# Three widths instead of four for TensorE's branches in the experts' products

## The chip, the cores and the metric

The kernel runs on one core of a Trainium2 chip. The metric is the device time of one execution in microseconds (us). Three runs of the kernel before took 733.88, 737.55 and 741.72 us; the median is 737.55 us. The execution that the profiler recorded took 735.24 us, of which 733.3 us lie between its first and its last instruction (the span).

## The reference, cut to what matters

Three parts follow each other. All data are 32-bit floats.

1. An attention over 4 batches, 8 heads, 576 positions and 64 values a head: a local one (each position sees the keys less than 4 away) plus one on fourfold averaged positions. Its result is x, 2304 tokens by 512.
2. A dense block without a gate: `h = ((x @ w1) * (x @ w2)) @ w3`, then `x = h @ w_out`.
3. A routed block with 8 experts, one expert a token:

```
logits = x @ w_gate                      # 2304 x 8
e_idx  = argmax(logits, axis=1)          # each token's one expert
gate_w = softmax(logits)[e_idx];  eom = sigmoid(x @ w_output_gate)
for e in range(8):
    mask = e_idx == e
    h  = relu(x[mask] @ w1[e])           # 512 -> 1024
    ye = h @ w2[e]                       # 1024 -> 512
    out[mask] = gate_w[mask] * eom[mask, e] * ye
```

How many tokens an expert gets is known only while the kernel runs.

## The kernel before, in words

**Stages.** The first 460 us or so make the attention, the dense block and the routing tables; the attention's small steps are spread between the matrix products. Then come the experts, from about 477 us to the end.

**Precision.** A product of two 32-bit matrices is made as three TensorE products of split operands: high by high, high by low, low by high (`mm3`, L419 to L421; `mm3n`, L425 to L427). Each of the three is one weight load (PEld) and one matmul (PE). The splitting is a cast on ScalarE (L775) and a subtraction on VectorE or GpSimd (L777).

**Experts by rank.** `route_rank` sorts the experts by their count. The program has eight ranks, and a rank r has a fixed capacity `CAPS[r]` in token columns: 352, 336, 320, 304, 288, 288, 272, and 384 for the last one, rank 7, which is the fullest expert. Tokens over a capacity are handled after the loop by `overflow`. The weights of a rank's expert are read by an address held in a register (`ew_load`, SP's queue), 4 MB a rank in eight transfers.

**First and second product.** `ga_pair(r, f0)` makes two of the eight 128-row parts of `relu(x @ w1)` for rank r: 2 parts x 4 slices of the inner dimension x 3 = 24 matmuls on one column range. `gb_step(r, dc)` makes one of the four 128-row parts of the second product: 8 slices x 3 = 24 matmuls. Ranks 1 to 7 call `ga_pair` four times each, ranks 0 to 6 call `gb_step` four times each (rank 7 ends with another form, `gb_rows`): 56 calls. I call the code of one such call a block. Rank 0's first product has no branches and lies before the loop.

**The branches.** Each block is made by `by_width`. It reads the rank's true count into a register of TensorE once a rank (`value_load`, L647), and writes the same 24 matmuls several times into the program, once for each entry of `CUTS`: for the full capacity C and for C less 16, 32 or 48 columns. Only the copy (arm) that the count calls for is executed. The first matmul of an accumulation always covers C columns, to clear the rest of the accumulator; the others have the arm's width.

```
CUTS = tuple(range(0, 64, 16))                       # L39
...
def arm(a, b):                                       # in by_width, from L649
    if b - a == 1:
        products(C - CUTS[a])
        return
    m = (a + b) // 2
    with tc.If(rt["n"][r] > C - CUTS[m]) as cond:    # L654
        arm(a, m)
    with cond.Else():
        arm(m, b)

arm(0, len(CUTS))
```

The branches are instructions of TensorE's queue alone; no other engine sees them. The order in the program is: compare with C-32; compare with C-16, arm C, jump to the end, arm C-16, jump to the end; compare with C-48, arm C-32, jump to the end, arm C-48. A count within 16 of C, or within 32 of it, costs two compares and one jump to the end; a smaller one costs two compares, both of which jump.

**Order.** From rank 0's second product on, the order of all five queues is written out by hand (`manual_schedule`): the second product of rank r, its blocks mixed with the transposes (L750) that prepare rank r+1's tokens, then the first product of rank r+1, its blocks mixed with the transposes of rank r's result (L861) and its scatter to the output (L851). ScalarE and VectorE take each block's result out of PSUM (L803 after the first product, L845 after the second). The weights of the coming ranks are loaded and split meanwhile.

Of the kernel before, what the change touches and what calls it, by code (L numbers as in the profile page):

```python
# [35 lines left out]
NBLK = [-(-c // P) for c in CAPS]  # L36
NBM = max(NBLK)
CMAX = max(CAPS)
CUTS = tuple(range(0, 64, 16))  # L39
NEG = -1e30  # L40
OOB = 1.0e6
RING = 2 * G
# [7 lines left out]
def attention_moe_kernel(ctx: ExitStack, tc: tile.TileContext, q, k, vw_in, v4_in, w1, w2, w3, w_out,  # L50
# [594 lines left out]
    def by_width(r, C, products):  # L645
# [3 lines left out]
        def arm(a, b):  # L649
# [11 lines that stand above are left out]
# [534 lines left out]
```

## Time and profile before

| What | Value |
|---|---|
| Median of three runs | 737.55 us (733.88 to 741.72) |
| Profiled execution | 735.24 us, span 733.3 us |
[...]
| TensorE matmuls busy | 687.4 us, 94% of the span |
| TensorE weight loads busy | 655.7 us, 89% (they overlap the matmuls) |
| VectorE, ScalarE, GpSimd busy | 382.6, 287.3 and 330.8 us |

The busy time of an engine is the union of its instructions; what is left of a stretch is idle time. In the view by stretches the columns are the stretch from:to, its length, the busy time of PE, PEld, DVE, ACT and POOL with the number of instructions, the granted clock, the busy share of the DMA engines and GB/s. A rank's stretch there runs from the start of its first product (rank 0: second) to the start of the next rank's, in us from the start of the span. "Idle before <- releaser" names what the profile takes for the end of the wait. Where an instruction waits for several semaphores, it names the one that moved last, which need not be the one that was waited for. Branches, register loads and waits are instructions of the sequencer that feeds an engine. They are not counted as busy, but their durations are recorded (PEldq is the sequencer of TensorE), and the sequencer runs ahead of its engine.

### The profile page before, as it was taken

The page shows a single profiled execution, that of the slowest core. Times are in us where ns is not written, and L with a number is a line of the kernel's source. Part 1 is how long each engine was busy: PE and PEld are TensorE (multiplying, and loading weights), DVE is VectorE, ACT ScalarE, POOL GpSimd, SP SyncE. Part 2 cuts the span into 40 slices and gives each one's busy share as a digit, 9 for nine tenths or more (in the row PEclk, how much of TensorE's full clock was granted, in tenths as well). Part 3 has the DMA queues.
Part 4 walks back from the last instruction along what each step waited for, and adds up shares of the span by engine and source line. Part 5 has one row for each costly group of instructions (what it writes and reads, how often), then busy time and mean ns, then how long its engine had stood idle before and what let it go on. Part 6 is the DMA issues. An engine that isn't in the chain of part 4 may idle for free.

```text
span 733.3 us, 14894 instructions
## 1 busy us (share of the span) xinstructions
PE 687.4 (94%) x5710; PEld 655.7 (89%) x5711; DVE 382.6 (52%) x887; ACT 287.3 (39%) x664; POOL 330.8 (45%) x339
## 2 busy tenths in 40 slices
PE   5689999999999999999999999989999998988995
PEld 3589989899999999999999999979989998987994
DVE  8889889854544545443243434462733445535340
ACT  3446435562543245145122120444444534544520
POOL 6868468763662255141011120243545546557331
PEclk9999999999999999999999999989999999999998
DMA  8879645463342043111100101573645647557301
GB/s 328 239 247 299 217 122 189 129 177 116 98 136 82 22 117 95 44 40 44 44 22 1 44 1 59 200 250 89 203 135 188 212 149 238 175 179 237 122 29 42
DMA packets 38297, 98.26 MB, mean 134 GB/s; under 512 B 6018, under 2 KB 12930, under 8 KB 38192
## 3 DMA queue, kind: packets, MB, share of 16 engines
q1 hardware_dynamic: 34768, 86.82, 37.4%
q0 software_dynamic: 3424, 9.93, 3.6%
q8 instruction: 79, 1.29, 0.7%
q14 instruction: 26, 0.21, 0.1%
HBM read 84.93 MB, written 12.29 MB: 133 GB/s over the span
## 4 chain that ended last, share of the span: by engine, by line
PE 67%; issue 9%; DVE 9%; POOL 7%; DMA 5%; ACT 1%; SPq 0%; POOLq 0%; DVEq 0%; ACTq 0%
PE g L419 14%; PE g L421 14%; PE g L420 14%; PE g L425 6%; PE g L426 5%; PE g L427 5%; POOL W L777 2%; PE at L282 2%; POOL out_dram L851 2%; DVE cv L139 2%; DMA v<-in_v_dram 1%; DVE cv L140 1%; PE at L210 1%; DMA kz<-in_k_dram 1%; DVE wf L141 1%
## 5 line engine op out<-in xcount | busy, mean ns | idle before, releaser
L419 PE MATMUL g<-xh,W 128*128 128x384 f32 x384 | 131.9, 343 | 0.6 <-ACT a L453 0.6
L421 PE MATMUL g<-xh,W 128*128 128x384 f32 x384 | 129.2, 337 | 0.8 <-POOL W L398 0.8
L420 PE MATMUL g<-xl,W 128*128 128x384 f32 x384 | 129.2, 336 | 0.0
L777 POOL TENSOR_TENSOR W<-raw,W 128x1024 fp32r<-128x1024 f32 x29 | 70.8, 2441 | 89.6 <-ACT W L775 89.6
L458 POOL TENSOR_TENSOR h<-a,h 128x384 fp32r<-128x384 f32 x30 | 30.5, 1018 | 100.3 <-ACT h L456 100.3
L419 PEld LDWEIGHTS g<-xh,W 128*128 128x128 f32 x384 | 72.1, 188 | 2.3 <-ACT a L453 1.2
L421 PEld LDWEIGHTS g<-xh,W 128*128 128x128 f32 x384 | 72.1, 188 | 1.7 <-POOL W L398 1.6
L425 PE MATMUL g<-xT,W 128*128 128x288 f32 (+5 forms) x224 | 68.8, 307 | 4.9 <-ACT W L775 3.2
L425 PE MATMUL g<-h,W 128*128 128x320 f32 (+7 forms) x224 | 68.4, 305 | 5.4 <-ACT xT L754 2.1
L420 PEld LDWEIGHTS g<-xl,W 128*128 128x128 f32 x384 | 72.2, 188 | 0.1
L419 PE MATMUL g<-wc,h 128*128 128x272 f32 (+1 forms) x240 | 68.7, 287 | 0.0
L420 PE MATMUL g<-wc,h 128*128 128x272 f32 (+1 forms) x240 | 68.3, 286 | 0.0
L421 PE MATMUL g<-wc,h 128*128 128x272 f32 (+1 forms) x240 | 67.8, 285 | 0.0
L427 PE MATMUL g<-xT,W 128*128 128x320 f32 (+4 forms) x224 | 66.4, 296 | 0.9 <-issue 0.9
L426 PE MATMUL g<-h,W 128*128 128x320 f32 (+4 forms) x224 | 66.1, 295 | 0.8 <-DVE h L803 0.8
L426 PE MATMUL g<-xT,W 128*128 128x320 f32 (+4 forms) x224 | 66.3, 296 | 0.0
L427 PE MATMUL g<-h,W 128*128 128x320 f32 (+4 forms) x224 | 66.0, 295 | 0.3 <-issue 0.3
L775 ACT CAST W<-raw 128x1024 fp32r<-128x1024 f32 x61 | 63.2, 1047 | 4.0 <-DMA raw<-in_moe_w_dram 4.0
L777 DVE TENSOR_TENSOR W<-raw,W 128x1024 fp32r<-128x1024 f32 x32 | 43.3, 1352 | 37.3 <-ACT W L775 37.3
L454 DVE TENSOR_TENSOR a<-g,a 128x384 f32<-128x384 f32 x48 | 26.7, 555 | 55.3 <-PE g L421 47.3
L803 DVE SCALAR_TENSOR_TENSOR h<-g,h 128x288 fp32r<-128x288 f32 (+6 forms) x64 | 30.9, 486 | 36.9 <-ACT h L803 35.9
L803 ACT ACTIVATE h<-g 128x288 fp32r<-128x288 f32 (+6 forms) x64 | 28.0, 437 | 55.3 <-PE g L427 49.6
(266 smaller groups left out, 1735.9 us busy)
## 6 DMA issues: line engine op xcount, KB each, us to landing
raw<-in_moe_w_dram SPq DMA_DIRECT2D x61, 512.0 KB, 3.5
f64w<-in_moe_w_dram SPq DMA_DIRECT2D x16, 512.0 KB, 5.2
f<-in_moe_w_dram SPq DMA_DIRECT2D x16, 512.0 KB, 3.4
vw<-in_vw_dram SPq DMA_DIRECT2D x16, 384.0 KB, 4.0
kc<-in_k_dram SPq DMA_DIRECT2D x16, 288.0 KB, 3.7
qT<-in_q_dram SPq DMA_DIRECT2D x16, 288.0 KB, 4.3
kz<-in_k_dram SPq DMA_DIRECT2D x32, 144.0 KB, 3.5
v<-in_v_dram SPq DMA_DIRECT2D x16, 288.0 KB
```

Of the source, the lines that this page charges most:

```text
L139: nc.vector.tensor_scalar(c, hi, 3, 0x3FFFFFF8, op0=ALU.logical_shift_left, op1=ALU.bitwise_and)
L419: nc.tensor.matmul(ps, whi, xhi, start=first, stop=False)
L420: nc.tensor.matmul(ps, whi, xlo, start=False, stop=False)
L421: return nc.tensor.matmul(ps, wlo, xhi, start=False, stop=last)
L425: nc.tensor.matmul(ps[:, 0:w], whi, xhi[:, 0:w], start=first, stop=False)
L426: nc.tensor.matmul(ps[:, 0:n], whi, xlo[:, 0:n], start=False, stop=False)
L427: nc.tensor.matmul(ps[:, 0:n], wlo, xhi[:, 0:n], start=False, stop=last)
L454: nc.vector.tensor_tensor(a, pp[1][:, 0:G], a, op=ALU.mult)
L458: eng.tensor_tensor(lo, a, hi.bitcast(F32), op=ALU.subtract)
L775: nc.scalar.copy(out=hi, in_=t)
L777: ins = eng.tensor_tensor(lo, t, hi.bitcast(F32), op=ALU.subtract)
L803: return nc.scalar.activation(out=t[:, 0, 0:C], in_=ps[:, 0:C], func=AF.Relu), nc.vector.scalar_tensor_tensor(t[:, 1, 0:C], ps[:, 0:C], 0. ...
```

## The change

```
--- before
+++ after
-CUTS = tuple(range(0, 64, 16))
+CUTS = (0, 16, 48)
```

The list has three entries instead of four; `by_width` is the same text. With three entries `arm` splits 1 and 2: compare with C-16; arm C, jump to the end; compare with C-48, arm C-16, jump to the end; arm C-48. The copy for C-32 columns is gone from each of the 56 blocks, and with it one compare and one jump. A count within 16 of C now costs one compare and one jump to the end; the others cost what they did. A count from 32 to 47 columns under C, which had its own arm, now takes arm C-16.

## Rows read from the trace of the kernel before

**Rows 1.** Page: span; engine, busy us (share of the span), instructions.
```profile
span 733.3 us, 14894 instructions
...
PE 687.4 (94%) x5710; PEld 655.7 (89%) x5711; DVE 382.6 (52%) x887; ACT 287.3 (39%) x664; POOL 330.8 (45%) x339
```

**Rows 2.** Busy time in eight stretches, one a rank, ranks 0 to 7.
```profile
493.30:509.80 16.50, 16.50 (x110) 16.44 (x109) 3.62 (x5) 6.09 (x10) 4.51 (x2) 1.00 0.25 74
509.80:543.70 33.90, 31.69 (x218) 30.72 (x217) 18.51 (x43) 14.32 (x23) 16.51 (x11) 1.00 0.52 167
543.70:574.60 30.90, 30.90 (x218) 30.59 (x217) 12.69 (x18) 14.11 (x23) 16.04 (x10) 1.00 0.58 181
574.60:604.80 30.20, 29.96 (x218) 29.22 (x216) 13.79 (x18) 13.90 (x23) 17.30 (x11) 1.00 0.53 184
604.80:631.80 27.00, 24.76 (x216) 24.50 (x217) 12.36 (x18) 13.85 (x23) 15.48 (x11) 1.00 0.63 200
631.80:661.40 29.60, 25.71 (x219) 24.55 (x217) 12.37 (x18) 14.54 (x25) 17.68 (x11) 1.00 0.55 184
661.40:690.50 29.10, 25.37 (x216) 24.49 (x217) 12.91 (x18) 13.20 (x22) 14.95 (x10) 1.00 0.58 190
690.50:708.00 17.50, 17.50 (x110) 17.31 (x110) 9.35 (x13) 8.43 (x13) 10.78 (x6) 1.00 0.27 91
```

**Rows 3.** Matmul groups by shape, 490 to 709 us: count | busy, mean ns | idle before.
```profile
L426 PE MATMUL g<-h,W 128*128 128x320 f32 x64 | 19.9, 311 | 0.8 <-DVE h L803 0.8
L426 PE MATMUL g<-xT,W 128*128 128x320 f32 x64 | 19.7, 309 | 0.0
L426 PE MATMUL g<-xT,W 128*128 128x240 f32 x64 | 17.6, 276 | 0.0
L426 PE MATMUL g<-xT,W 128*128 128x368 f32 x32 | 10.6, 331 | 0.0
L426 PE MATMUL g<-h,W 128*128 128x352 f32 x32 | 10.3, 321 | 0.0
L426 PE MATMUL g<-xT,W 128*128 128x304 f32 x32 | 9.7, 302 | 0.0
L426 PE MATMUL g<-xT,W 128*128 128x224 f32 x32 | 8.7, 272 | 0.0
```

**Rows 4.** Line L654, the branches: all; ranks 0, 2, 3, 5: ns min/median/max, first and last start.
```profile
L654 PEldq COMPARE_BRANCH  x144: 65/208/3362, 490.4 to 705.0; - x144
...
L654 PEldq COMPARE_BRANCH  x10: 65/68/393, 494.6 to 507.0; - x10
...
L654 PEldq COMPARE_BRANCH  x24: 65/65/677, 544.6 to 573.5; - x24
...
L654 PEldq COMPARE_BRANCH  x22: 65/65/2568, 575.5 to 602.1; - x22
...
L654 PEldq COMPARE_BRANCH  x16: 208/208/2833, 633.0 to 659.3; - x16
```

**Rows 5.** PE in order of time at three gaps [idle before <-releaser].
```profile
606.89 0.40 PE L425 MATMUL g<-xT,W 128*128 128x288 f32 x1 [2.11 <-ACT W L775]
...
654.15 0.37 PE L425 MATMUL g<-h,W 128*128 128x288 f32 x1 [1.06 <-ACT xT L754]
...
681.37 0.39 PE L425 MATMUL g<-h,W 128*128 128x272 f32 x1 [1.38 <-issue]
```

**Rows 6.** Line L654 just before those three gaps.
```profile
L654 PEldq COMPARE_BRANCH  x2: 214/1788/3362, 603.2 to 603.5; - x2
...
L654 PEldq COMPARE_BRANCH  x1: 2733/2733/2733, 650.9 to 650.9; - x1
...
L654 PEldq COMPARE_BRANCH  x1: 3188/3188/3188, 677.9 to 677.9; - x1
```

**Rows 7.** Chain of work that ended last: start, us, what.
```profile
606.18 0.71 issue
```

**Rows 8.** Page: DMA queue, kind: packets, MB, share of 16 engines.
```profile
q8 instruction: 79, 1.29, 0.7%
```

## The prediction

> **What bounds the kernel now.** I read the page first. TensorE's matmuls are busy 94% of the span [rows 1], so time is gained only where a matmul is shortened or a gap before one is closed. The change touches the experts' stage alone, so the second view is busy time by stretches there, one stretch a rank [rows 2]. Length less PE busy is the idle time of the rank: 0.00, 2.21, 0.00, 0.24, 2.24, 3.89, 3.73 and 0.00 us for ranks 0 to 7, together 12.31 us. The clock is granted in full throughout, so it plays no part. The reader is to see that the idle time sits mostly in ranks 4 to 6 (9.86 us), and that these are the ranks with the shortest blocks.
>
> The third view is the matmuls by shape, to see which arms are taken [rows 3]. In the first product (out of xT) each of ranks 1 to 7 shows 32 matmuls of L426: 64 of 320 columns, 32 of 304, 64 of 240, 32 of 224, 32 of 368. With the capacities there is one solution: 368 is 384-16; 224 is 272-48; both of 240 are 288-48; 304 is rank 3's full 304, and then the two of 320 are 336-16 and 320-0. Rank 0's second product has its full 352. **No rank takes the arm of C-32**, so every matmul keeps its width.
>
> The fourth view is the branch line by itself [rows 4]. Of 144 branches half take 208 ns or less, but the longest takes 3362 ns. In rank 2 none is over 677 ns, and rank 2 has no idle time; in ranks 3 and 5 the longest take 2568 and 2833 ns. The last view puts gaps beside branches. PE's gaps of 2.11, 1.06 and 1.38 us end at 606.89, 654.15 and 681.37 [rows 5]; just before them branches of 3362, 2733 and 3188 ns, begun at 603.5, 650.9 and 677.9, end at 606.8, 653.6 and 681.1 [rows 6]. Two of those gaps have ScalarE as their releaser, but the chain shows that the first of them ran on 0.71 us with nothing seen to wait for [rows 7]. So I take the branch as the cause, and the releaser as a semaphore that happened to move late. 0.8 us is another thing, a wait for VectorE inside rank 1's second product [rows 3]. That leaves 11.5 us for branches and what stalls like them.
>
> Why would a branch take 3 us? TensorE's code is long: 11,421 matmuls and weight loads that ran [rows 1] and 56 blocks x 3 arms x 48 that did not, 19,485. The instruction queue q8 moved 1.29 MB in 79 packets [rows 8]: 66 bytes for each of these, 16.3 KB a packet. So **the arms that are not taken are fetched too**, and a packet is used up after about 247 instructions. A block has 192 matmuls and loads in its four arms, 6 branches and mostly 8 for a transpose, 206 in all: 1.20 blocks a packet. PE needs per block (busy time by 8 blocks, by 4 for ranks 0 and 7) 4.13, 3.96, 3.86, 3.75, 3.10, 3.21, 3.17 and 4.38 us, so a packet lasts 4.9, 4.8, 4.6, 4.5, 3.7, 3.9, 3.8 and 5.2 us. Beside the idle times this is an order: none at 4.9 and over, on average 0.54 at 4.5 to 4.8 (rank 1 without VectorE's 0.82: 1.39, 0, 0.24), 3.3 at 3.7 to 3.9. My reading: code arrives about every 4 to 5 us, and a rank that uses it faster waits at the branch that leads into the next packet.
>
> [...]
>
> **The change part by part.**
>
> *The arm that goes.* 48 matmuls and loads and 2 branches fall out of each block: 206 becomes 156, or 1.58 blocks a packet. A packet then lasts 4.9, 5.1 and 5.0 us in ranks 4 to 6 and 5.9 to 6.3 in ranks 1 to 3. Ranks 1 to 3 come to where ranks 0 and 7 have no idle time: I take their remaining 1.63 us as gone. Ranks 4 to 6 come to rank 0's pace, a little slower than that of ranks 1 to 3 now; by the order above 0 to 0.54 us a rank would stay. The cover is thinner there, though: the sequencer runs ahead of PE by some matmuls, which last less in narrow ranks. The 3362 and 3188 ns stalls showed 2.11 and 1.38 us, so 1.3 and 1.8 us were hidden. I therefore keep 1.0 us a rank, 3.0 us. Sum: 11.5 - 3.0 = **8.5 us gained**. Bounds: at most all 11.5; at least, if waits fall only as the code does (50 of 206, 24%), 2.8.
>
> *The compare that goes.* Blocks at full width (ranks 0, 2 and 3: 4 + 8 + 8) have one compare less, 20 x 65 ns = 1.3 us of the sequencer. Counted at nothing: queued matmuls cover it, since ranks 0 and 2 have no idle time with it. Without that cover it would be a gain of 1.3. The blocks at C-16 and C-48 execute as many branches as before.
>
> [...]
>
> *The arm that is missed.* It costs nothing here. Were a rank to need it, 16 columns more would cost about 0.94 us (rank 2's 30.90 busy against rank 3's 29.96).
>
> *What is late next.* Weights, casts and splits would have to follow ranks 4 to 6 at about 25 us. After its gap, from 606.89 to 631.80, rank 4 already ran 24.91 us with 24.76 busy, and the weights of rank 5 were loaded and split beside it, at 63% of the DMA engines, 15.5 us of GpSimd and 13.9 of ScalarE. So I add nothing. The 25 us after the last branch have none of this code, and are unchanged.
>
> **The sum.** 735.24 - 8.5 = 726.7 us for an execution like the profiled one, which is 2.3 us under the median of the runs. The same -1.16% on 737.55 gives 729.0.
>
> **The rivals.**
>
> *Only in proportion.* The waits are set by how long a packet takes behind weight transfers on the DMA engines (a share of 0.53 to 0.63 in ranks 3 to 6), and each remaining packet stalls as before. Then 24% of 11.5 us goes, 2.8: 732.4, on the median 734.7. For it: rank 3, at 4.5 us a packet, still has a 2568 ns branch, so lateness varies. Against it: the steep step between 3.9 and 4.5 us.
>
> *Nothing.* The gaps belong to ScalarE's casts, as the releasers say, and a long branch only waits with them. Then 735.2, on the median 737.5. For it: the named releasers. Against it: 681.37 has no releaser, and the 0.71 us.
> [...]
>
> *Slower: the place of the seams.* Every block moves against the packet's ends. If it is this, and not the rate, that decides which ranks wait, ranks 4 to 6 could all pay rank 5's 3.89 and rank 4's opening 2.11, 18.0 together instead of 9.86: 8.1 us slower, 743.3. It decides once a stall at a rank's opening repeats in each narrow rank. For it: rank 4 has hardly a gap after its opening although its blocks are rank 5's. Against it: fewer packets leave fewer seams.
>
> **How the numbers follow.** Forecast 0.64, in proportion 0.21, nothing 0.11, slower 0.04. Within the forecast the gain runs from 5.5 to 11.5 us; a change of 1% (about what a measurement of this kernel tells from none) is 7.4, so some four fifths of it is faster by more: 0.51. The rest of it, the second and the third case are within 1%: 0.45. Slower 0.04. The range: all 11.5 us gone is -1.56%, 726.0, and single runs lie 0.5% under their median, so 722.5 below; above, the proportional case, 734.7, and a little for the runs' scatter, 735.5.
>
> **What would show it.** Right: q8 falls to about 68 packets (56 x 50 x 66 bytes less is 0.18 MB, 11 packets); the same counts of each matmul width; 124 branches instead of 144; idle time by rank near 0 in ranks 1 to 3 and around 1 us in ranks 4 to 6; few branches over 2 us. Wrong: fewer packets but long branches and gaps as before (the rate is not the cause), gaps that stay where no branch is long (ScalarE or the weights), or new gaps in ranks that had none (the seams). The size is wrong if ranks 4 to 6 keep 2 us or more each.

## The result, and the profile after

The changed kernel takes 728.43 us (median of 19 runs, 725.12 to 732.17) against 737.14 us for the kernel before (19 runs, 731.48 to 743.97). The ratio is 0.9889, with a 95% interval from 0.9866 to 0.9913. The forecast was 729.0 us, or -1.16%. The execution that the profiler recorded took 732.17 us, span 730.1. It is one of the slowest of its 19, and its experts' stage began 5.4 us later than in the profile of before (498.7 against 493.3 us), so spans are not to be compared; the stage is.

First the page of the changed kernel, the same two lines as [rows 1] and [rows 8].

```profile
span 730.1 us, 14874 instructions
...
PE 690.3 (95%) x5710; PEld 659.1 (90%) x5711; DVE 381.6 (52%) x887; ACT 286.1 (39%) x664; POOL 332.4 (46%) x339
...
q8 instruction: 68, 1.11, 0.6%
```

The matmuls and weight loads are as many as before, 20 instructions fewer ran (the compares), and q8 moved 68 packets instead of 79. Now the busy time by rank, ranks 0 to 7, which answers to [rows 2] line by line.

```profile
498.70:515.20 16.50, 16.50 (x111) 16.44 (x110) 3.62 (x5) 6.09 (x10) 4.54 (x2) 1.00 0.30 96
515.20:547.30 32.10, 31.27 (x217) 30.71 (x217) 18.53 (x43) 14.12 (x23) 16.23 (x11) 1.00 0.54 175
547.30:578.20 30.90, 30.90 (x219) 30.59 (x218) 12.22 (x18) 14.02 (x23) 16.29 (x11) 1.00 0.56 180
578.20:607.70 29.50, 29.50 (x217) 29.25 (x217) 12.69 (x18) 13.90 (x23) 17.10 (x11) 1.00 0.57 187
607.70:633.80 26.10, 24.81 (x218) 24.44 (x217) 12.48 (x18) 13.75 (x23) 16.33 (x11) 1.00 0.64 209
633.80:661.00 27.20, 25.12 (x218) 24.54 (x218) 12.27 (x18) 13.56 (x23) 17.12 (x11) 1.00 0.61 196
661.00:687.40 26.40, 24.63 (x218) 24.33 (x217) 12.76 (x18) 13.96 (x23) 16.27 (x11) 1.00 0.63 208
687.40:704.90 17.50, 17.50 (x111) 17.31 (x110) 9.36 (x13) 8.44 (x13) 10.72 (x6) 1.00 0.29 89
```

Length less PE busy gives idle times of 0, 0.83, 0, 0, 1.29, 2.08, 1.77 and 0 us, 5.97 in all, where it was 12.31. The eight stretches last 206.2 us together, against 214.7: **8.5 us less**, the whole of the gain. The idle time accounts for 6.3 of these. The other 2.2 stand under "busy" (202.39 before, 200.23 now), and that is a matter of reading: in an unbroken stream a matmul of a narrow rank starts every 0.11 us and its record lasts 0.28 us (the changed kernel at 621.26, 621.37 and 621.48), so each gap hides some 0.17 us behind the last record before it. The stage had 16 gaps before and has 6 now; ten times 0.17 us is an estimated 1.7 of the 2.2. A sum of gaps understates stalls by so much.

What is left of idle time shows in the view of the waits, PE in the stage: who waited for whom, us in total, times, longest.

```profile
PE g L427 <- POOL W L777: 3.9, 3, 1.3
PE g L426 <- DVE h L803: 0.8, 1, 0.8
PE g L425 <- ACT xT L754: 0.8, 1, 0.8
PE g L425 <- issue: 0.5, 1, 0.5
```

The last two are the old kind. In front of the 0.8 (ACT xT) stands the only branch of the changed kernel that took over 0.5 us; in the kernel before 16 took over 1 us. The 0.5 has no long branch and lies in the middle of an arm. The first is new: three gaps of 1.3 us, one in each of ranks 4, 5 and 6, in the first block of the second product, where a matmul reads a weight that GpSimd has only just split. So the waits for code fell from 11.5 to 1.2 us of idle time, and **a wait for GpSimd of 3.9 us has come in**. The two branch rows, all of line L654 and the one before 654.97 us (ns min/median/max, first and last start), answer to [rows 4] and [rows 6].

```profile
L654 PEldq COMPARE_BRANCH  x124: 65/208/2475, 495.9 to 701.9; - x124
...
L654 PEldq COMPARE_BRANCH  x1: 2475/2475/2475, 652.3 to 652.3; - x1
```

That the long branches wait for code can be read directly, since the traces have the start and the length of every packet of q8. All 16 branches of over 1 us in the kernel before end 1.28 to 1.53 us after such a packet has landed; so does the one of the changed kernel, and in all traces of this case together 104 of 105 end 1.28 to 1.56 us after one. The changed kernel's three waits for GpSimd end 3.9 to 4.3 us after the last packet.

### The profile page after: what moved, and what is told of

It is laid out like the page before. It is cut to its first block, busy times and chain, and to the rows that moved or that the text cites. A ratio compares the mean times of both kernels' runs of the same rounds, so it can differ in the third digit from the quotient of the medians.

```text
span 730.1 us, 14874 instructions
## 1 busy us (share of the span) xinstructions
PE 690.3 (95%) x5710; PEld 659.1 (90%) x5711; DVE 381.6 (52%) x887; ACT 286.1 (39%) x664; POOL 332.4 (46%) x339
## 4 chain that ended last, share of the span: by engine, by line
PE 52%; issue 18%; POOL 16%; DMA 7%; DVE 6%; ACT 1%; SPq 0%; POOLq 0%; DVEq 0%; ACTq 0%
PE g L419 14%; PE g L421 13%; PE g L420 13%; POOL W L777 6%; POOL out_dram L851 3%; POOL xr L732 2%; DMA v<-in_v_dram 2%; PE at L282 2%; DMA vw<-in_vw_dram 1%; PE g L427 1%; PE at L222 1%; PE g L425 1%; DVE cv L140 1%; PE g L426 1%; PE at L278 1%
## 5 line engine op out<-in xcount | busy, mean ns | idle before, releaser
L777 DVE TENSOR_TENSOR W<-raw,W 128x1024 fp32r<-128x1024 f32 x32 | 41.4, 1294 | 38.0 <-ACT W L775 33.2
```

What stands on the lines that cost most here:

```text
L777: ins = eng.tensor_tensor(lo, t, hi.bitcast(F32), op=ALU.subtract)
```

## The experiments

Two questions were open. Was it the amount of code that made the branches slow, or their number, or the place of the packets' ends? And what brought the new wait? All ratios are against the kernel before on the same chip.

**The split moved to VectorE (three arms).**

```
-        eng = nc.vector if i % 2 != (r == 0 and m == 1) or (r == 0 and m == 0) else nc.gpsimd
+        eng = nc.vector if i % 2 != (r == 0 and m == 1) or (r == 0 and m == 0) or (r > 0 and m == 1 and i == 2) else nc.gpsimd
```

> The changed kernel, with the third split of each second weight matrix (ranks 1 to 7) on VectorE instead of GpSimd. Theory A (code supply was the old bound, and what is left is mostly GpSimd's late split): the three waits of 1.3 us in the second products of ranks 4, 5 and 6 go, 3.9 us in all; idle time of TensorE in the experts' stage falls from 6.0 to about 2 us, the time by about 4 us against the changed kernel, to a ratio of about 0.983 against the kernel before. Rival B (GpSimd's split is only the last of several things that are late together): the gaps stay within 1 us of 3.9 us under another releaser, ratio 0.989.

Measured: 721.12 us, ratio 0.9804 (0.9754 to 0.9855). The stretches of ranks 4 to 6:

```profile
602.30:627.00 24.70, 24.70 (x218) 24.45 (x217) 13.42 (x19) 13.73 (x23) 13.99 (x10) 1.00 0.63 221
627.00:652.40 25.40, 24.86 (x219) 24.46 (x218) 13.32 (x19) 13.68 (x23) 14.68 (x10) 1.00 0.60 210
652.40:676.60 24.20, 24.20 (x219) 24.16 (x218) 13.71 (x19) 13.94 (x23) 13.86 (x10) 1.00 0.65 227
```

The three waits are gone and nothing took their place: 0.54 us is all the idle time of the stage, which lasts 199.7 us. Theory A holds, and more than the 3.9 us went: rank 1's 0.8 us wait for VectorE is gone too. VectorE's order of time tells why, here of the changed kernel and of this run:

```profile
525.98 3.03 DVE L893 TENSOR_SCALAR b_b<-b_b 128x18 f32<-128x18 f32 x1
```

```profile
521.72 0.18 DVE L893 TENSOR_SCALAR b_b<-b_b 128x18 f32<-128x18 f32 x1
```

The small instruction took 3.03 us where GpSimd's split for rank 1 ran beside it (526.53 to 528.97) and 0.18 us without that split. In every trace with the split on GpSimd one instruction of VectorE is held up like this, L893 (3.00 us in the kernel before) or in the next run L892, and in none of those with the split on VectorE. This version is faster than both kernels.

**The unused arm shortened (four arms, all branches).**

```
-                products(C - CUTS[a])
+                products(C - CUTS[a], CUTS[a] == 32)    # short: 3 matmuls instead of 24
```

> The kernel before with all four arms and all its compares and jumps, but the arm of C-32, which no rank takes, holds 3 matmuls instead of 24 (a count that needed it would get a wrong product). Theory A (the amount of code between the arms counts): like the changed kernel, about 70 packets on q8, 144 branches of which at most three are over 1 us, idle time in the stage 5 to 8 us, ratio 0.987 to 0.993. Rival C (the number of compares and jumps counts): like the kernel before, long branches and 11 to 14 us of idle time, ratio 0.997 to 1.003.

Measured: 726.11 us, ratio 0.9877 (0.9828 to 0.9925), as the changed kernel. The packets, the branches, and the waits of PE in the stage:

```profile
q8 instruction: 70, 1.15, 0.7%
```

```profile
L654 PEldq COMPARE_BRANCH  x144: 65/200/2270, 490.6 to 696.6; - x144
```

```profile
PE g L427 <- POOL W L777: 4.2, 3, 1.6
PE g L426 <- DVE h L803: 1.4, 1, 1.4
PE g L425 <- ACT h L803: 0.4, 1, 0.4
```

All 144 branches ran, and only two took over 1 us. The code stalls are down to 0.4 us, and the same wait for GpSimd has come in. So the gain is that of the code left out; the compares and jumps are worth nothing that these intervals show. Rival C falls.

**A fifth arm that no rank takes.**

```
-CUTS = tuple(range(0, 64, 16))
+CUTS = tuple(range(0, 80, 16))
```

> The kernel before with a fifth arm, C-64, that no rank takes: the same arms run, and the ranks at C-48 pass three compares instead of two. Theory A: about 90 packets on q8, 0.97 blocks a packet, so a packet lasts 3.0 us in ranks 4 to 6 and 3.7 us in ranks 1 to 3; ranks 1 to 3 get idle times like those of ranks 4 to 6 before (about 3 us each), and ranks 4 to 6 are held to about 4 us a packet, 7 to 9 us of idle time each; together 30 to 40 us instead of 12, ratio 1.02 to 1.04. Rival C: 24 compares of 0.2 us more, mostly hidden, ratio 1.00 to 1.005. Rival D (the place of the packets' ends): anything from 0.99 to 1.01.

Measured: 757.48 us, ratio 1.0292 (1.0235 to 1.0350), 90 packets. The stretches of ranks 0 to 7:

```profile
495.30:511.80 16.50, 16.50 (x110) 16.44 (x109) 3.63 (x5) 6.09 (x10) 4.56 (x2) 1.00 0.23 75
511.80:544.10 32.30, 31.47 (x217) 30.74 (x216) 18.53 (x43) 14.32 (x23) 16.20 (x11) 1.00 0.54 175
544.10:581.60 37.50, 31.84 (x219) 30.61 (x218) 12.47 (x18) 14.09 (x23) 16.26 (x11) 1.00 0.48 150
581.60:612.40 30.80, 30.09 (x217) 29.14 (x215) 13.80 (x18) 14.16 (x24) 17.37 (x11) 1.00 0.56 181
612.40:642.30 29.90, 26.30 (x216) 24.59 (x216) 12.01 (x18) 14.32 (x25) 16.80 (x10) 1.00 0.55 185
642.30:677.70 35.40, 29.13 (x216) 27.54 (x216) 11.91 (x18) 12.91 (x22) 16.25 (x10) 0.90 0.47 152
677.70:713.50 35.80, 27.43 (x216) 26.46 (x217) 13.05 (x18) 13.93 (x23) 17.16 (x10) 0.95 0.51 164
713.50:731.00 17.50, 17.50 (x110) 17.31 (x110) 9.35 (x13) 8.43 (x13) 9.18 (x5) 1.00 0.21 73
```

The ratio is as theory A had it; code that never runs makes the stage 21.0 us longer. The idle time is not what I expected: 25.4 us instead of 30 to 40, and ranks 1, 2 and 3 with 0.83 (all of it VectorE), 5.66 and 0.71 us, where I had about 3 for each. Idle time is only 13.1 of the 21.0 us; the rest stands under "busy", part of it for a slower clock (last section). So the pace tells the sum only roughly, and not which rank pays. Nor are the stalls all at branches. After 634.5 us no branch takes over 0.41 us:

```profile
L654 PEldq COMPARE_BRANCH  x84: 65/208/406, 634.3 to 728.0; - x84
```

Yet TensorE still stands idle for 15.7 us there, 11.8 of them in front of matmuls in the middle of an arm.

**The packets' ends moved, before and after.** One dead arm, C-64, in the very first block.

```
-        by_width(r, C, products)
+        by_width(r, C, products, tuple(range(0, 80, 16)) if (r, dc) == (0, 0) else CUTS)
```

> The kernel before with one dead arm (C-64, never taken) in the very first block only: every later block lies about 50 instructions, a fifth of a packet, further on, and nothing else changes. Theory A: idle time in the stage 10 to 15 us, spread otherwise but still mostly in ranks 4 to 6, ratio 0.997 to 1.003. Rival D (the place of the packets' ends decides, not the rate): the idle time moves by more than 5 us either way, ratio under 0.993 or over 1.007.

> The kernel with one dead arm in the first block once more, which showed 8.2 us of idle time in its first profile. If the shifted packet ends are worth 4 us: 7 to 9.5 us again, gaps at the same blocks. If that profile was a lucky execution: 10 to 13 us.

> The changed kernel with one dead arm (C-64, never taken) in the very first block only, so that all later packet ends lie elsewhere. Theory A (rate): idle time in the stage 5 to 8 us, of which 3.9 is GpSimd's split, ratio 0.986 to 0.992 against the kernel before. Rival D (the changed kernel owes its gain to a lucky place of the packets' ends): idle time of 9 us or more, ratio over 0.993.

Measured, four arms: 733.84 us (the kernel before: 735.55), ratio 1.0002 (0.9969 to 1.0036), idle time 8.2 us in the first profile and 8.8 in the second. Three arms (the dead arm makes four in that block): 727.85 us, ratio 0.9880 (0.9838 to 0.9923), idle time 4.5 us. The waits of PE in the stage of the latter:

```profile
PE g L427 <- POOL W L777: 3.1, 3, 1.3
PE g L426 <- DVE h L803: 0.8, 1, 0.8
PE g L425 <- ACT h L803: 0.5, 1, 0.5
```

With three arms the place of the ends hardly matters: code stalls stay at 0.5 us. With four arms it does something: both profiles have about 3.5 us less idle time than those of the kernel before, which neither theory expected, but the timed runs show no gain, and their interval allows 2.3 us at most. That contradiction stays open. In the one other place of the ends that was run, the gain of the change is the same.

**The kernel before once more.**

> The kernel before once more, for the scatter of the idle time between executions. If the stalls follow the code's layout: 11 to 13.5 us of idle time in the stage, the large gaps at the same blocks as in the first profile. If they follow chance among the transfers: a total that differs by 3 us or more, or large gaps at other blocks.

Measured: one execution, 739.47 us, 12.1 us of idle time, against 12.3. The large gaps come at ranks 1 and 4 to 6 again and at the opening of rank 4, of rank 6 and of rank 6's second product, as in the first profile, but their sizes differ (1.1 us at rank 4's opening, where it was 2.1), and rank 4 has three gaps (0.97, 0.21 and 1.68 us) where it had one of 0.15. My reading, which no run tests by itself: layout sets where stalls can be, the transfers at the moment set how long they are. Neither expectation is quite met.

**The split on VectorE, four arms.** The same edit as in the first experiment, in the kernel before.

> The kernel before (four arms) with the third split of each second weight matrix on VectorE, as in the run that gained with three arms. Theory A (GpSimd's split becomes late only once code arrives in time): no more than the 0.8 us of rank 1's VectorE wait goes; idle time in the stage stays at 9 to 14 us, ratio 0.997 to 1.002. Rival E (the two costs are independent and add): 3.9 us or more are gained here too, ratio about 0.991.

Measured: 732.07 us, ratio 0.9942 (0.9914 to 0.9970), idle time 8.9 us. This is more than theory A had and less than rival E's. Rank 1's stretch shows where most of it is from:

```profile
511.40:542.90 31.50, 31.29 (x219) 30.77 (x218) 16.82 (x44) 14.32 (x23) 13.81 (x10) 1.00 0.56 179
```

Its idle time is 0.21 us against 2.21 before: not only VectorE's 0.82 is gone, but 1.2 of the 1.39 us of code stalls that followed it. My reading is that the 0.82 us wait had emptied the queue that covered the next stalls, and had put off the fetch of the next code: the packet that ended the first of them began 9.0 us after its predecessor, and here 7.1. No run tests that by itself. Ranks 3 to 6 keep 8.7 us, and no matmul waits for GpSimd's split there, as none did before. So with four arms GpSimd's split is never late enough to be waited for, as theory A says, and what the edit gained here is another wait. The timed intervals are too wide to say whether the two edits add up.

**Fewer arms still.** Three arms with the split on VectorE; each rank keeps the full arm and the one that this input takes.

```
     def by_width(r, C, products):
+        CUTS = {0: (0,), 1: (0, 16), 2: (0,), 3: (0,), 7: (0, 16)}.get(r, (0, 48))
```

> Three arms with the split on VectorE, and each rank keeps only the full arm and the one that this input takes (ranks 0, 2 and 3 one arm and no branch, the others two; other counts would get correct but wider products). Theory A: with 0.5 us of idle time left in the experts' stage there is nothing more for less code to give: about 53 packets, idle time 0 to 0.6 us, ratio 0.977 to 0.983, the same as the run with three arms and the split on VectorE (0.980). If less code went on paying (fetches disturbing the weights' transfers, for example): 3 us or more beyond that, ratio under 0.976.

Measured: 723.51 us, ratio 0.9815 (0.9777 to 0.9852), 53 packets, and no idle time of TensorE at all in the stage (198.8 us). The time is that of the run with 68 packets (721.12 us): where code left 0.54 us of idle time at most, less of it gave no time that these intervals show. For an input with other counts it would be slower.

**An eighth of the weight transfers, four arms.** The splits repeat that eighth, so the engines' work is the same and the products are not the reference's.

```
+        if r > 0:
+            ins = nc.sync.dma_start(out=t[:, 0:128], in_=(e_w2 if m else e_w1)[bass.ds(reg, 1), P * i:P * i + P, 0:128]...)
...
+            t = t[:, 0:128].unsqueeze(1).to_broadcast([P, 8, 128])
```

> The kernel before (four arms), where ranks 1 to 7 load only an eighth of each weight transfer (128 of 1024 columns, 64 KB instead of 512) and the splits repeat that eighth; so the weights and the output are not the reference's, and the work of the engines is the same. Theory F (a packet of code comes late because it queues behind weight transfers on the DMA engines): 79 packets and 144 branches as before, but few branches over 1 us, idle time in the stage 1 to 4 us, ratio 0.983 to 0.990. Theory G (a packet takes this long by itself, the weights do not matter): 10 to 13 us of idle time, long branches as before, ratio 0.995 to 1.003.

Measured: 728.76 us, ratio 0.9894 (0.9836 to 0.9952). Packets of code, all branches, and ranks 4 to 6:

```profile
q8 instruction: 79, 1.29, 0.7%
```

```profile
L654 PEldq COMPARE_BRANCH  x144: 65/208/2151, 492.2 to 697.0; - x144
```

```profile
605.40:630.60 25.20, 25.18 (x217) 24.64 (x218) 11.75 (x18) 12.79 (x22) 15.43 (x10) 1.00 0.24 73
630.60:656.70 26.10, 24.81 (x218) 24.43 (x217) 12.36 (x18) 13.68 (x23) 17.04 (x11) 1.00 0.22 64
656.70:682.60 25.90, 24.49 (x219) 24.27 (x218) 12.85 (x18) 13.96 (x23) 16.38 (x11) 1.00 0.24 74
```

With all the code of before, 4 branches instead of 16 took over 1 us, and of 4.5 us of idle time only 0.9 is for code; 2.7 are GpSimd's split, which comes in here too, and 0.8 VectorE's wait. Theory F holds: a packet of code is late because of the weight transfers. Its own transfer is not slower for them: in the stage a packet of q8 took 1.06 us on average before and 1.07 us here. So the delay lies ahead of the transfer.

## Why the prediction was right, step by step

**The bound.** Right. The idle time of the experts' stage was what could be had; the widths of the matmuls did not change (the counts by shape are those of [rows 3]).

**The reading of the gaps.** Right. The gaps named after ScalarE [rows 5] were the branches' [rows 6]: with the same casts in the same order they went when dead code was taken out of the unused arm.

**Code and its pace.** Right in kind: 68 packets, 124 branches, almost no long ones. "Waits at the branch" was too narrow: without VectorE's wait the stage had 15 gaps before; 5 of them, 2.5 us, have no branch over 0.5 us in front of them, and the one of 0.94 us before 671.67 us lies in the middle of an arm, 1.6 us after a packet of code landed. In the trace after, ranks 1 to 3 lost all their code stalls, as forecast. Ranks 4 to 6 kept 1.2 us together where I had kept 3.0. The order of idle time by us a packet was too neat: the five arms put 5.66 us on one rank and none on its neighbour of nearly the same pace.

**Which waits remain.** The rival "in proportion" was wrong in its number but had the better account of the lateness: with light weight transfers the four arms hardly stall (0.9 us of idle time). The amount of code decided here how often a packet was needed (68, 79 and 90 packets with three, four and five arms), the weights how late it came, and a long stall needed both: less of either alone took the branches of over 1 us from 16 to 1, or to 4. A branch took up to 3.4 us [rows 4], but the stalls were not at branches alone: inside an arm, where no branch is, they reach 0.94 us before and 3.23 us with five arms.

**The compare that goes.** Counted at nothing, and nothing it was: the short arm kept all the compares and gained as much, as far as the intervals tell.

**What is late next.** This step failed: "So I add nothing" should have been 3.9 us. I took rank 4's 24.91 us after its opening gap as proof that weights and splits keep that pace. But it had been helped by the gap. GpSimd's order of time in the changed kernel, and the matmul that reads the split:

```profile
617.50 1.03 POOL L851 DMA_INDIRECT out_dram<-orow,b_si  x1 [0.30 <-issue]
618.84 1.75 POOL L851 DMA_INDIRECT out_dram<-orow,b_si  x1 [0.30 <-DVE orow L850]
620.60 2.39 POOL L777 TENSOR_TENSOR W<-raw,W 128x1024 fp32r<-128x1024 f32 x1
...
623.04 0.38 PE L427 MATMUL g<-h,W 128*128 128x240 f32 x1 [1.29 <-POOL W L777]
```

and in the kernel before:

```profile
613.66 1.02 POOL L851 DMA_INDIRECT out_dram<-orow,b_si  x1 [0.30 <-issue]
615.25 1.01 POOL L851 DMA_INDIRECT out_dram<-orow,b_si  x1 [0.56 <-PE g L427]
616.26 2.44 POOL L777 TENSOR_TENSOR W<-raw,W 128x1024 fp32r<-128x1024 f32 x1
```

```profile
621.16 0.28 PE L427 MATMUL g<-h,W 128*128 128x240 f32 x1
```

Before, the split ended at 618.70, 0.9 us before its block began (619.57) and 2.5 us before its matmul; now at 622.99, 3.0 us after the block began (620.00). While TensorE stood still for 2.11 us at the rank's opening, ScalarE's cast and GpSimd's queue behind it (splits, gathers and scatters in one order) had gone ahead: GpSimd's split before this one began 0.3 us after the rank's first matmul then, and 2.6 us after it now. That is 2.3 of the 3.9 us by which the split came later against its block. Another 1.2 us went in GpSimd's own queue, where a gather and a scatter that overlapped a split on VectorE took 1.79 and 1.75 us instead of 0.99 and 1.01. A pace that was seen just after a stall is no proof of that pace.

**The sum.** Forecast 8.5, stage 8.5; but by terms that balance: 10.3 us of code stalls gone rather than 8.5, 2.2 us that gaps do not show, and 3.9 us given back to GpSimd, 8.6. The mechanism was right, the agreement to a tenth is chance.

## What to carry to other kernels

In this kernel, copies of a loop body that a branch skips were not free: they were fetched too (68 packets against 79 and 90), and late beside the weight transfers. With three skipped copies to one executed, TensorE stood idle for 11.5 us at the jump or in the code behind it, with two for 1.2 us, and with three and an eighth of the weights for 0.9 us. Look at the branch line's longest durations beside the gaps of the engine, and do not trust the releaser of a gap that ends with a long branch. A gap inside an arm can be the same stall, as the one before 671.67 was; the landing of the code packets tells. Before calling a gap gain, ask what the other engines did during it: a stall also gives a late helper its time (2.3 us here), and the next gain may be one split moved to another engine, as here.

## What the runs showed of the hardware that was not expected

In the run with five arms a gap of 3.23 us in rank 5's first product [idle before <-releaser] was followed by half clock, as the busy time by stretches shows (the granted clock is the third number from the end).

```profile
655.54 0.36 PE L425 MATMUL g<-xT,W 128*128 128x240 f32 x1 [3.23 <-issue]
```

```profile
651.70:655.20 3.50, 0.61 (x6) 0.53 (x5) 0.46 (x1) 0.36 (x1) 3.37 (x2) 0.93 0.77 304
655.20:658.50 3.30, 2.96 (x15) 2.73 (x15) 1.05 (x2) 1.34 (x2) 0.00 (x0) 0.50 0.54 168
```

After 3.5 us with 0.61 us of matmuls the granted clock was 0.50 in the next stretch, of 3.3 us. Rank 5's matmuls were busy 29.13 us in that run against 25.71 before [rows 2], so an estimated 3 us of its loss are the clock's. The length of a gap alone does not tell it: in the same run gaps of 2.91 us (before 556.99) and 2.24 us (before 692.86) left the clock at 1.00, and one of 1.84 us (before 709.24) was followed by 0.50.
